# Tile 0 of x in two column parts, and the first key step between its transposes

## The chip, the cores and the metric

The kernel runs on one core of a Trainium2 chip. A core has a matrix engine (TensorE, PE in the profile; PEld is its weight load), a vector engine (VectorE, DVE), ScalarE (ACT), GpSimd (POOL) and SyncE (SP), which here only issues transfers. SP and ACT each have a queue of transfers. The metric is the device time of one execution in microseconds; before the change it is 190.84 us, the median of 5 runs (190.61 to 191.13).

## The reference

Two linear-attention blocks A and B read the same x (2048 rows, 640 columns, bf16) with weights of their own, and a gate mixes them row by row. The reference, cut to what matters:

```python
x = A_x
g = sigmoid((x * gate_w).sum(-1))
def block(x, wqkv, wo):                    # H = 32 heads of 20
    q, k, v = split_heads(x @ wqkv)
    phi = lambda t: where(t > 0, t + 1, exp(t)) + 1e-6
    pq, pk = phi(q), phi(k)
    kv, z = einsum("bhsd,bhse->bhde", pk, v), pk.sum(s)
    o = (pq @ kv) / ((pq * z).sum(-1) + 1e-6)
    return heads_joined(o) @ wo
out = g * block(x, A_wqkv, A_wo) + (1 - g) * block(x, B_wqkv, B_wo)
```

## The kernel before

x is cut into 16 tiles of 128 rows, and its 640 columns into 5 chunks of 128. The matrix engine needs x with columns on the partitions (XT), so every tile is transposed: tiles 0 and 1 on TensorE, against an identity matrix that comes with the constants (x_tp, L432 to L462: five products into PSUM, L438, in three pieces of 1, 2 and 2 columns, each followed by a copy to XT on VectorE, L453), and the tiles from 2 on by transposing transfers. The stages are: the keys of all tiles and both blocks (k_step, L485: for one tile, block and chunk a product with 512 weight columns, L491, and one with the other 128, L492; five steps make a tile's keys, then k_post applies phi), the products of keys with x (g_unit, L612), the queries (q_unit, L738), small products for the heads, and the output (o_mm, L905).

The order of the work: TensorE runs what it is given in the order written. For the other engines a planner (Sched, L75) walks through the work with estimated costs and lets each engine take, among the operations that can start, the one that can start first. It also assigns the 8 PSUM banks: a key step's result takes two neighbouring banks, a transposed piece one, the dummy products one. The first loads of a queue keep the order written (chain, L342). Each waiting operation waits for semaphores of what it needs, right before it is issued.

The start, which the change touches:

- ACT's queue (L395, L396): the constants with the identity (46 KB), then the gate's weights (1.2 KB).
- SP's queue (L397 to L413): x tile 0, key weights of A chunk 0, x tile 1, key weights of A chunks 1 to 4, then those of B, then the transposing loads, the rest of x and the other weights. Each of the first ones has 160 KB.
- TensorE (L548 to L559): six dummy products of ones with 512 columns (warm, L421), which nothing reads; the five transposes of tile 0; key step of tile 0, chunk 0; the five transposes of tile 1; the key steps of tile 0 chunk 1, tile 1 chunk 0, tile 1 chunk 1; the small transpose of the gate's weights (gate_col, L466); and then the steps of chunks 2 to 4 for both tiles.

The code of that order:

```python
    warm(6)
    pss = [Buf("k", "ps", 2) for _ in range(2)]
    x_tp(0)
    k_step("A", 0, 0, pss[0])
    x_tp(1)
    k_step("A", 0, 1, pss[0])
    k_step("A", 1, 0, pss[1])
    k_step("A", 1, 1, pss[1])
    gate_col()
```

Of the kernel before, what the change touches and what calls it, by code (L numbers as in the profile page):

```python
# [6 lines left out]
ACT = mybir.ActivationFunctionType  # L7
# [4 lines left out]
D = 640  # L12
# [62 lines left out]
class Sched:  # L75
# [7 lines left out]
    def op(self, eng, fn, cost, ins=(), outs=(), after=(), prio=None, name="", dma=None):  # L83
        o = Op(eng, fn, cost, list(ins), list(outs), after, len(self.ops) if prio is None else prio, name, dma)
        self.ops.append(o)
        return o
# [165 lines left out]
def body(nc, A_x, A_wqkv, A_wo, B_x, B_wqkv, B_wo, gate_w, out, log=None):  # L252
    x = A_x[0]
# [8 lines left out]
    XN = sb("XN", [128, NT, XS_W], bf)  # L262
# [54 lines left out]
    ONE = sb("ONE", [128, 128], bf)  # L317
# [10 lines left out]
    op = sch.op  # L328

    def psw(b, w):  # L330
        return PS[:, b.slot : b.slot + b.n, :].rearrange("p a b -> p (a b)")[:, 0:w]
# [3 lines left out]
    def dma(q, name, dst, src, nbytes, ins=(), outs=(), after=(), issue=450.0, transpose=False, prio=None):  # L335
        def fn(e):
            d = dst() if callable(dst) else dst
            with nc.allow_non_contiguous_dma(reason="layout"):
                return e.dma_start(d, src() if callable(src) else src, transpose=transpose)  # L339

        o = op(q, fn, 0.0, ins, outs, after, prio=prio, name=name, dma=(issue, nbytes, 95.0 if transpose else 330.0))
        if loading:  # L342
            o.behind = chain.get(q)
            chain[q] = o
        return o

    def mm_cost(n):
        return n / 2.4 + 2.5

    def act_cost(n):  # L350
        return 190 + 0.833 * n

    def dve1(n):
        return 155 + 1.04 * n
# [5 lines left out]
    bxn = [Buf("xn%d" % t) for t in range(NT)]  # L360
    bxt = [Buf("xt%d" % t) for t in range(NT)]
    bwk = {(X, c): Buf("wk%s%d" % (X, c)) for X in XS for c in range(NC)}
    bcst, bone, beps, bgwb = Buf("cst"), Buf("one"), Buf("eps"), Buf("gwb")
# [6 lines left out]
    bxo = Buf("xo")  # L370
    op("POOL", lambda e: e.memset(XN[:, :, D : D + 1], 1.0), 200.0, outs=[bxo], name="xones")

    def ld_x(q, t):
        dma(q, "x%d" % t, XN[:, t, 0:D], x[128 * t : 128 * t + 128, :], 163840, outs=[bxn[t]])

    def ld_wk(q, X, c, after=()):
        dma(q, "wk%s%d" % (X, c), WK[X][:, c, 0:D], wqkv[X][128 * c : 128 * c + 128, D : 2 * D], 163840, outs=[bwk[X, c]], after=after)
# [15 lines left out]

    bgw = Buf("gw5")
    dma("ACT", "cst", CST[:, :], cap[:, :], 128 * CW * 2, outs=[bcst])  # L395
    dma("ACT", "gw", GW5[:, :], gate_w.rearrange("(c p) -> c p", p=128), 1280, outs=[bgw])  # L396
    for c in range(NC):  # L397
        if c < 2:
            ld_x("SP", c)
        ld_wk("SP", "A", c)  # L400
    for c in range(NC):
        ld_wk("SP", "B", c)
# [15 lines left out]

    bw = Buf("warm", "ps")

    def warm(n):  # L421
        for i in range(n):
            op(
                "PE",
                lambda e: e.matmul(psw(bw, 512), ONE[:, :], ONE[:, :].unsqueeze(1).to_broadcast([128, 4, 128]), start=True, stop=True),
                430.0,
                ins=[bone],
                outs=[bw],
                name="warm",
            )  # L430

    def x_tp(t):  # L432
        for lo, hi in ((0, 1), (1, 3), (3, 5)):
            bt = Buf("tp", "ps")
            for c in range(lo, hi):
                op(
                    "PE",
                    lambda e, c=c, lo=lo, bt=bt: e.matmul(  # L438
                        PS[:, bt.slot, 128 * (c - lo) : 128 * (c - lo) + 128],
                        XN[:, t, 128 * c : 128 * c + 128],  # L440
                        IDN,
                        start=True,
                        stop=True,
                    ),
                    100.0,
                    ins=[bxn[t], bcst],
                    outs=[bt],
                    name="tp%d" % t,
                )
            half = Buf("xth")  # L450
            op(
                "DVE",
                lambda e, lo=lo, hi=hi, bt=bt: e.tensor_copy(  # L453
                    XT[:, lo:hi, 128 * t : 128 * t + 128],
                    PS[:, bt.slot, 0 : 128 * (hi - lo)].rearrange("p (c s) -> p c s", c=hi - lo),
                ),
                dve1(128 * (hi - lo)),
                ins=[bt],
                outs=[half],
                name="tpc%d" % t,  # L460
            )
            bxt[t].parts = getattr(bxt[t], "parts", []) + [half] * (hi - lo)  # L462
# [20 lines left out]
    bpk = {}  # L483

    def k_step(X, t, c, ps):  # L485
        w = D + 1 if X == "B" else D

        def fn(e):
            a = psw(ps, w)
            l = XT[:, c, 128 * t : 128 * t + 128]  # L490
            e.matmul(a[:, 0:512], l, WK[X][:, c, 0:512], start=(c == 0), stop=(c == NC - 1))  # L491
            return e.matmul(a[:, 512:w], l, WK[X][:, c, 512:w], start=(c == 0), stop=(c == NC - 1))  # L492

        xin = [bxt[t].parts[c] if hasattr(bxt[t], "parts") else bxt[t]]
        op(
            "PE",
            fn,
            mm_cost(512) + mm_cost(128),
            ins=xin + [bwk[X, c]] + ([bgc] if X == "B" else []),
            outs=[ps],  # L500
            name="k%s%d_%d" % (X, t, c),
        )
# [39 lines left out]
    def k_unit(X, t):  # L542
# [2 lines left out]
            k_step(X, t, c, ps)  # L545
        k_post(X, t, ps)

    warm(6)  # L548
    pss = [Buf("k", "ps", 2) for _ in range(2)]
    x_tp(0)  # L550
    k_step("A", 0, 0, pss[0])
    x_tp(1)
    k_step("A", 0, 1, pss[0])
    k_step("A", 1, 0, pss[1])
# [13 lines left out]
    for t in range(2, NT):  # L568
# [12 lines left out]
        ins=[bgg, bge2] + bge,  # L581
        outs=[bgg2],
        prio=LOW + 52,
        name="gm",
# [9 lines left out]
    for i, X in enumerate(XS):  # L594
        for j in range(NB):
# [8 lines left out]
                ins=bgd,  # L604
                outs=[b],
# [6 lines left out]
    def g_unit(X, g, fill):  # L612
        ps = Buf("g", "ps", 2)
        i = XS.index(X)
        for t in range(NT):

            def fn(e, t=t):
                a = psw(ps, D + 1)
                l = PKt[X][:, t, g::5]
                e.matmul(a[:, 0:512], l, XN[:, t, 0:512], start=(t == 0), stop=(t == NT - 1))  # L620
                return e.matmul(a[:, 512 : D + 1], l, XN[:, t, 512 : D + 1], start=(t == 0), stop=(t == NT - 1))  # L621

            op("PE", fn, mm_cost(512) + mm_cost(128), ins=[bxn[t], bxo, bpk[X, t]], outs=[ps], name="g%s%d_%d" % (X, g, t))
            if t % 4 == 3 and t < NT - 1:
                fill(t // 4)
        b, z = Buf("gt"), Buf("zbd")
        bgs[X, g] = Buf("gs%s%d" % (X, g))
        bz[X, g] = z
        op("ACT", lambda e: e.activation(GTS[X][:, g, :], psw(ps, D), ACT.Copy), act_cost(D), ins=[ps], outs=[b], name="gc")
        op(  # L630
            "DVE",
            lambda e: e.tensor_copy(ZC[:, NC * i + g : NC * i + g + 1], psw(ps, D + 1)[:, D : D + 1]),
            170.0,
            ins=[ps, b],
            outs=[z],
            name="zc",
        )
        dma(
            "SP",
            "gs%s%d" % (X, g),  # L640
            GS[X][:, :, 128 * g : 128 * g + 128],
            GTS[X][:, g, :],
            163840,
            ins=[b],
            outs=[bgs[X, g]],
            issue=850.0,
            transpose=True,
        )
# [343 lines left out]
    for g in range(NC):  # L992
        g_unit("A", g, lambda k: q_next(1))
# [28 lines left out]
    for g in range(NC):  # L1022
        g_unit("B", g, fill_b(g))
        q_next((2, 2, 1, 0, 0)[g])
# [35 lines left out]
def bass_gated_mix__linear_attn_block__linear_attn_block__prompt_kernel(nc, *args):  # L1060
    body(nc, *args)
# [28 lines left out]
```

## Time and profile before

| what | us |
|---|---|
| median of 5 runs | 190.84 (190.61 to 191.13) |
| the profiled execution's own time | 190.56 |
| its span, first to last instruction | 189.3 |
| TensorE busy | 184.3 (97%) |
| VectorE busy | 127.4 (67%) |
| ScalarE busy | 95.7 (51%) |
| first transpose of tile 0 | at 3.58 |
| first key step | at 4.37 |
| first transpose of tile 1 | at 4.98 |

The profile is of one execution. A line of the order of time gives the start, the time covered, engine, line of the kernel, operation, what is written and read, how many instructions, and in brackets how long the engine was idle before and what ended that. "SPq" and "ACTq" are the issues of transfers. A product's listed time reaches to the end of its result, so that two products in a row overlap; their pace is read from the distance of their starts. "To landing" is the time from the issue of a transfer to its last completion.

### The profile page before, as it was taken

The numbers are of one execution on the slowest core, as the hardware profiler recorded it, in microseconds if no ns is written. First come the engines' busy times: TensorE is split into PE (matmuls) and PEld (weight loads), VectorE is DVE, ScalarE is ACT, GpSimd is POOL, SyncE is SP. The second block draws the span as 40 slices with busy tenths as digits, with TensorE's granted clock in tenths as the row PEclk, the third lists the DMA queues.
The fourth block names the chain that finished last, engine by engine and source line by source line (L and its number), as shares of the span: only waits on it lengthen the run. The fifth ranks groups of instructions, "written<-read, shape, count | busy, mean of one in ns | idle before, by whom it ended". The sixth has DMA issues, their size and how long they took to land.

```text
span 189.3 us, 3195 instructions
## 1 busy us (share of the span) xinstructions
PE 184.3 (97%) x1245; PEld 107.9 (57%) x1269; DVE 127.4 (67%) x251; ACT 95.7 (51%) x171; POOL 0.4 (0%) x6
## 2 busy tenths in 40 slices
PE   7999999999999999999999999999999999999995
PEld 2555555555555566656557556655666555555552
DVE  2489888888833546478787689888996936865300
ACT  2255555656554545545584777876624875000112
POOL 0000000000000000000000000000000000000000
DMA  5979999997013011013010005430020153233222
GB/s 159 294 144 189 197 389 367 361 226 161 5 48 101 1 37 35 0 35 31 7 27 8 3 5 142 113 95 5 1 51 16 26 168 93 73 137 107 104 73 69
DMA packets 29469, 19.42 MB, mean 103 GB/s; under 512 B 17390, under 2 KB 29198, under 8 KB 29454
## 3 DMA queue, kind: packets, MB, share of 16 engines
q1 hardware_dynamic: 29300, 19.17, 38.4%
q8 instruction: 10, 0.16, 0.3%
q10 hardware_dynamic: 154, 0.05, 0.1%
q14 instruction: 5, 0.04, 0.1%
HBM read 9.95 MB, written 2.64 MB: 67 GB/s over the span
## 4 chain that ended last, share of the span: by engine, by line
PE 96%; DMA 2%; issue 1%; SPq 0%; DVE 0%; DVEq 0%
PE ps L913 23%; PE ps L743 22%; PE ps L620 18%; PE ps L491 18%; PE ps L492 5%; PE ps L621 5%; PE ps L661 2%; DMA XN<-in_A_x_dram 2%; PE ps L697 1%; SPq L339 0%; PE ps L698 0%; PE ps L826 0%; PE ps L438 0%; DVE TSB L957 0%; PE ps L472 0%
## 5 line engine op out<-in xcount | busy, mean ns | idle before, releaser
L491 PE MATMUL ps<-WKW,XT 128*128 128x512 bf16 x154 | 42.9, 379 | 0.2 <-DVE XT L453 0.2
L760 ACT ACTIVATE EK<-ps 128x512 bf16<-128x512 f32 x40 | 24.0, 599 | 31.3 <-PE ps L743 29.8
L492 PE MATMUL ps<-WKW,XT 128*128 128x128 bf16 (+1 forms) x160 | 35.1, 219 | 0.3
L524 ACT ACTIVATE EK<-ps 128x640 bf16<-128x640 f32 x32 | 22.3, 704 | 12.2 <-DVE EK L527 5.4
L491 PEld LDWEIGHTS ps<-WKW,XT 128*128 128x128 bf16 x160 | 15.6, 98 | 19.1 <-issue 0.4
L743 PE MATMUL ps<-XT,WQA 128*128 128x512 bf16 x96 | 24.0, 379 | 0.1
L743 PE MATMUL ps<-XT,WQB 128*128 128x512 bf16 x95 | 23.3, 379 | 0.4 <-issue 0.2
L620 PE MATMUL ps<-XN,PKB 128*128 128x512 bf16 x80 | 23.5, 379 | 0.0
L770 DVE TENSOR_SCALAR EK<-EK 128x512 bf16<-128x512 bf16 x40 | 11.7, 291 | 17.2 <-ACT EK L760 17.0
L620 PE MATMUL ps<-XN,PKA 128*128 128x512 bf16 x78 | 23.1, 379 | 0.1
L621 PE MATMUL ps<-XN,PKA 128*128 128x129 bf16 x80 | 17.6, 220 | 0.1
L621 PE MATMUL ps<-XN,PKB 128*128 128x129 bf16 x80 | 17.6, 220 | 0.0
L913 PE MATMUL ps<-WPA,EX 128*128 128x128 bf16 (+1 forms) x116 | 16.8, 296 | 0.2
L913 PE MATMUL ps<-WPB,PKA 128*128 128x512 bf16 (+1 forms) x118 | 16.4, 298 | 0.1
L743 PEld LDWEIGHTS ps<-XT,WQB 128*128 128x128 bf16 x100 | 10.9, 118 | 8.5 <-issue 0.2
L492 PEld LDWEIGHTS ps<-WKW,XT 128*128 128x128 bf16 x160 | 15.7, 98 | 0.0
L743 PEld LDWEIGHTS ps<-XT,WQA 128*128 128x128 bf16 x100 | 10.6, 117 | 8.1
L527 DVE TENSOR_SCALAR EK<-EK 128x640 bf16<-128x640 bf16 x32 | 10.4, 325 | 7.1 <-ACT EK L524 7.1
L959 ACT ACTIVATE TSB<-ps 128x640 bf16<-128x640 f32 (+1 forms) x4 | 2.7, 677 | 23.9 <-PE ps L913 23.9
L620 PEld LDWEIGHTS ps<-XN,PKA 128*128 128x128 bf16 x80 | 9.4, 117 | 7.9
L620 PEld LDWEIGHTS ps<-XN,PKB 128*128 128x128 bf16 x80 | 9.4, 118 | 7.8
L535 DVE SCALAR_TENSOR_TENSOR PKB<-ps,EK 128x640 bf16<-128x640 f32 x16 | 13.2, 825 | 0.6
(77 smaller groups left out, 230.9 us busy)
## 6 DMA issues: line engine op xcount, KB each, us to landing
out_dram<-TSB SPq DMA_DIRECT2D x15, 160.0 KB, 1.8
XN<-in_A_x_dram SPq DMA_DIRECT2D x1, 2240.0 KB, 9.1
WKW<-in_A_wqkv_dram SPq DMA_DIRECT2D x5, 160.0 KB, 3.2
WKW<-in_B_wqkv_dram SPq DMA_DIRECT2D x5, 160.0 KB, 3.9
WQA<-in_A_wqkv_dram SPq DMA_DIRECT2D x1, 800.0 KB, 10.7
WQB<-in_B_wqkv_dram SPq DMA_DIRECT2D x1, 800.0 KB, 13.5
WVA<-in_A_wqkv_dram SPq DMA_DIRECT2D x1, 800.0 KB, 12.8
WVB<-in_B_wqkv_dram SPq DMA_DIRECT2D x1, 800.0 KB, 14.3
```

The source lines that it names most:

```text
L491: e.matmul(a[:, 0:512], l, WK[X][:, c, 0:512], start=(c == 0), stop=(c == NC - 1))
L492: return e.matmul(a[:, 512:w], l, WK[X][:, c, 512:w], start=(c == 0), stop=(c == NC - 1))
L524: op("ACT", lambda e: e.activation(EK[:, ek.slot, :], psw(ps, D), ACT.Exp), act_cost(D), ins=[ps] + first, outs=[ek], name="ke")
L527: lambda e: e.tensor_scalar(EK[:, ek.slot, :], EK[:, ek.slot, :], 1.0, EPS, op0=ALU.min, op1=ALU.add),
L535: lambda e: e.scalar_tensor_tensor(PKt[X][:, t, :], psw(ps, D), 0.0, EK[:, ek.slot, :], op0=ALU.max, op1=ALU.add),
L620: e.matmul(a[:, 0:512], l, XN[:, t, 0:512], start=(t == 0), stop=(t == NT - 1))
L621: return e.matmul(a[:, 512 : D + 1], l, XN[:, t, 512 : D + 1], start=(t == 0), stop=(t == NT - 1))
L661: r = e.matmul(PS[0:GR, ps.slot, GR * i : GR * i + GR], WV[X][:, c, lo : lo + GR], gv[:, c, :, lo // 5 : lo // 5 + 24], start=(c == 0), st ...
L743: r = e.matmul(PS[:, ps.slot, :], WQ[X][:, c, g::5], XT[:, c, 512 * b : 512 * b + 512], start=(c == 0), stop=(c == NC - 1),)
L760: lambda e: e.activation(EQ[:, eq.slot, :], PS[:, ps.slot, :], ACT.Exp),
L770: lambda e: e.tensor_scalar(EQ[:, eq.slot, :], EQ[:, eq.slot, :], 1.0, EPS, op0=ALU.min, op1=ALU.add),
L913: r = e.matmul(a[:, l0 - lo : h0 - lo], PQ[X, b][:, g, 128 * (t % 4) : 128 * (t % 4) + 128], WP[X][:, g, l0:h0], start=(X == first and g = ...
```

## The change

Tile 0 of x is loaded in two column parts: columns 0 to 255 (64 KB) on SP's queue, in the place of the old load, and columns 256 to 639 (96 KB) on ACT's queue, between the constants and the gate's weights. The transposes of chunks 0 and 1 of tile 0 wait for the first part, those of chunks 2 to 4 for the second. Tile 0's transposes of chunks 2 to 4 are moved behind the key step of tile 0, chunk 0, and the pieces of both tiles become 1, 1 and 3 columns. Of the six dummy products four stay, and four of a quarter of the width (128 columns) follow them. The later product that reads tile 0 of x as a whole (g_unit, t = 0) is told of both parts.

```diff
     dma("ACT", "cst", CST[:, :], cap[:, :], 128 * CW * 2, outs=[bcst])
+    bx0 = Buf("xn0a")
+    dma("ACT", "x0b", XN[:, 0, 256:D], x[0:128, 256:D], 98304, outs=[bxn[0]])
+    dma("SP", "x0a", XN[:, 0, 0:256], x[0:128, 0:256], 65536, outs=[bx0])
     dma("ACT", "gw", GW5[:, :], gate_w.rearrange("(c p) -> c p", p=128), 1280, outs=[bgw])
     for c in range(NC):
-        if c < 2:
-            ld_x("SP", c)
+        if c == 1:
+            ld_x("SP", 1)
         ld_wk("SP", "A", c)
...
-    def warm(n):
+    def warm(n, w=4):
         for i in range(n):
             op(
                 "PE",
-                lambda e: e.matmul(psw(bw, 512), ONE[:, :], ONE[:, :].unsqueeze(1).to_broadcast([128, 4, 128]), start=True, stop=True),
-                430.0,
+                lambda e: e.matmul(psw(bw, 128 * w), ONE[:, :], ONE[:, :].unsqueeze(1).to_broadcast([128, w, 128]), start=True, stop=True),
+                107.0 * w,
...
-    def x_tp(t):
-        for lo, hi in ((0, 1), (1, 3), (3, 5)):
+    def x_tp(t, pieces=((0, 1), (1, 2), (2, 5))):
+        for lo, hi in pieces:
...
-                    ins=[bxn[t], bcst],
+                    ins=[bx0 if t == 0 and c < 2 else bxn[t], bcst],
...
-    warm(6)
+    warm(4)
+    warm(4, 1)
     pss = [Buf("k", "ps", 2) for _ in range(2)]
-    x_tp(0)
+    x_tp(0, ((0, 1), (1, 2)))
     k_step("A", 0, 0, pss[0])
+    x_tp(0, ((2, 5),))
     x_tp(1)
...
-            op("PE", fn, mm_cost(512) + mm_cost(128), ins=[bxn[t], bxo, bpk[X, t]], outs=[ps], name="g%s%d_%d" % (X, g, t))
+            op("PE", fn, mm_cost(512) + mm_cost(128), ins=[bxn[t], bxo, bpk[X, t]] + ([bx0] if t == 0 else []), outs=[ps], name="g%s%d_%d" % (X, g, t))
```

## The prediction

> **What bounds the kernel now.** I read the page first (busy times and the chain that ended last), then the order of time of the first six microseconds, then the stretches of half a microsecond with the DMA share, then the loads with their times to landing.
>
> ```profile
> span 189.3 us, 3195 instructions
> PE 184.3 (97%) x1245; PEld 107.9 (57%) x1269; DVE 127.4 (67%) x251; ACT 95.7 (51%) x171; POOL 0.4 (0%) x6
> PE 96%; DMA 2%; issue 1%; SPq 0%; DVE 0%; DVEq 0%
> ```
>
> TensorE is the bound nearly everywhere, and the 2% DMA of the chain lies at the start. So a change at the start is worth exactly the time by which it moves the point from which TensorE no longer waits. The order of time shows that point:
>
> ```profile
> 1.05 2.74 PE L425 MATMUL ps<-ONE 128*128 128x512 bf16 x6 [1.05 <-DVE ONE L368]
> 3.24 0.11 PEld L438 LDWEIGHTS ps<-CST,XN 128*128 128x128 bf16 x1 [0.36 <-DMA XN<-in_A_x_dram]
> 3.58 0.56 PE L438 MATMUL ps<-CST,XN 128*128 128x128 bf16 x5
> 3.94 0.95 DVE L453 CAST XT<-ps 128x128 bf16<-128x128 f32 x3 [2.94 <-PE ps L438]
> 4.37 0.38 PE L491 MATMUL ps<-WKW,XT 128*128 128x512 bf16 x1 [0.23 <-DVE XT L453]
> 4.59 0.22 PE L492 MATMUL ps<-WKW,XT 128*128 128x128 bf16 x1
> 4.97 0.28 PEld L438 LDWEIGHTS ps<-CST,XN 128*128 128x128 bf16 x5 [0.50 <-DMA XN<-in_A_x_dram]
> 4.98 0.45 PE L438 MATMUL ps<-CST,XN 128*128 128x128 bf16 x5 [0.17 <-DMA XN<-in_A_x_dram]
> 5.25 0.95 DVE L453 CAST XT<-ps 128x128 bf16<-128x128 f32 x3 [0.35 <-PE ps L438]
> 5.39 0.10 PEld L491 LDWEIGHTS ps<-WKW,XT 128*128 128x128 bf16 x1
> 5.40 0.39 PE L491 MATMUL ps<-WKW,XT 128*128 128x512 bf16 x1
> ```
>
> The five transposes of tile 0 start at 3.58, its first key step at 4.37. Then TensorE stands until x tile 1 has landed (4.97), transposes it, and stands once more before the key step of tile 0, chunk 1, whose weights load at 5.39. The five transposes of tile 1 are spaced 0.056, so they had left TensorE free from about 5.26. What came at 5.39 is the key weights of chunk 1, the fourth load of the SP queue:
>
> ```profile
> L339 SPq DMA_DIRECT2D WKW<-in_A_wqkv_dram x1: 432/432/432, 2.1 to 2.1; - x1
> DMA to landing us min/median/max: 3.2/3.2/3.2
> ```
>
> Issued at 2.12, landed 3.2 later: 5.35 or so, 0.04 before that weight load. Tile 1, issued at 1.64, landed 3.3 later, at 4.93. From 5.40 on TensorE is busy almost without a gap. So two loads of the SP queue, tile 1 and then chunk 1 of the key weights, set the end, and tile 0 doesn't.
>
> **Tile 0 in two parts.** The loads of the SP queue start 0.44 to 0.47 apart (0.74, 1.18, 1.64, 2.12). The first column part takes the old load's place and, with 128 rows as before, I give it the old issue time (0.39), so chunk 0's weights, tile 1 and chunk 1 are issued when they were. The second part goes to ACT's queue behind the constants, at 1.13. What it is moved past there: the gate weights (from 1.13 to about 1.55) and the table load (from 1.81 to about 2.25, 1.28 long). The first exponential is at 8.00; the gate weights are read at 6.32, and with the slowest of the early loads' times to landing (4.0) they would be there at 5.55. Both cost nothing; a landing later than 6.3 would cost its excess one for one.
>
> Does it move tile 1 and chunk 1? The bytes ahead of chunk 1's end are the same (46 of constants, then four times 160 KB). Stretches: length, busy time of each engine, clock, DMA share, GB/s.
>
> ```profile
> 2.00:2.50 0.50, 0.50 (x3) 0.18 (x2) 0.00 (x0) 0.50 (x1) 0.00 (x0) 1.00 0.90 276
> 2.50:3.00 0.50, 0.50 (x3) 0.15 (x1) 0.00 (x0) 0.50 (x1) 0.00 (x0) 1.00 1.05 375
> 3.00:3.50 0.50, 0.50 (x2) 0.11 (x1) 0.00 (x0) 0.10 (x1) 0.00 (x0) 1.00 1.12 159
> 3.50:4.00 0.50, 0.50 (x6) 0.38 (x4) 0.06 (x1) 0.00 (x0) 0.00 (x0) 1.00 0.62 143
> 4.00:4.50 0.50, 0.27 (x4) 0.13 (x2) 0.50 (x3) 0.00 (x0) 0.00 (x0) 1.00 0.95 318
> ```
>
> The engines are full from 2.0, and the slow stretch from 3.0 to 4.0 lies behind tile 0. Upper bound: 128 more packets, 8 for each of 16 engines, and one more completion each. In the first 9 us ACT's queue moved 154 packets, 0.05 MB, in 2.9% of 16 engines' time, 27 ns a packet; SP's moved 1961, 2.02 MB, in 75.7%, 56 ns. A line through these two (309 and 1030 bytes) leaves 15 ns for an empty packet: 9 times 15 is 0.13 us later. Lower bound: if a queue were a road of its own, SP's would carry 96 KB less ahead of tile 1, at 375 GB/s 0.26 us earlier. I take +0.1: a DMA share at or over 0.9 with 276 to 375 GB/s is what full engines look like, so packets and not queues should count.
>
> [...]
>
> **Shorter dummies.** Their starts are 0.43 apart (weight loads at 1.45, 1.88, 2.31, 2.73), so the sixth ends its issue at 3.58, just when the first transpose starts: tile 0 had landed by 3.24. Four long ones reach 2.73, four of a quarter 3.16. The first part lands between the constants' time (0.73 + 2.3 = 3.0) and the old load's (3.2). So transposes 0 and 1 start near 3.2, 0.4 earlier. The copy started 0.36 after the first transpose and the key step 0.43 after that: 3.99 now, and chunk 0's weights landed at 1.18 + 2.4 = 3.6. The key step issues in 0.28 (half pace: 0.55), the other three transposes in 0.17 (0.32): done at 4.44 (4.86). The second part, issued at 1.13, lands between 2.3 and 3.3 later, 3.4 to 4.4; at the late end the transposes end at 4.6. All are before 4.97. So the 0.4 us saved become a longer wait for tile 1: gain 0 on the path, and its cover is that wait.
>
> **Pieces and order.** Pieces of 1, 1 and 3 columns replace 1, 2 and 2. The copies took 292 and 415 ns for 128 and 256 columns, so I estimate 538 for 384. Tile 1: the three together end near 6.20 as before, and chunk 2 of tile 1 is read first at about 6.7: cost 0. Tile 0: its last copy starts some 0.27 after the last transpose, 4.66, and ends at 5.20, ahead of the copy of tile 1's first column at 5.25. In the half-pace case it ends near 5.56 and holds that copy, and so tile 1's first key step (5.68), up to 0.25: upper bound +0.2, I take 0. The wait on the first part that the diff adds to the later product of t = 0 is long over. PSUM still has a bank for every piece.
>
> **Sum.** The profiled execution took 190.56 (span 189.3 and 1.26 around it), 0.28 under the median of 190.84. 190.56 + 0.1 = 190.66; against the median 190.94, which I forecast, within 0.2% (0.38 us, about what a measurement can tell from no change). Own range: 190.84 - 0.26 to 190.84 + 0.13 + 0.2, so 190.6 to 191.2.
>
> **Rival 1, slower: TensorE's clock.** The dummies run 0.43 apart, later 512-column products 0.22; five transposes take 0.56 at 3.58 but 0.45 at 4.98. So the pace doubles inside the transposes of tile 0, some 2.8 us after the first dummy, although the granted clock reads 1.00 throughout. TensorE was busy from 1.05 to 4.1 without a break. Now it pauses from about 3.4 to 3.99. If that pause makes the doubling start anew, it comes at 3.99 + 2.8 = 6.8. The work from 5.40 to 6.8 then runs at half pace, +0.7, and tile 1's transposes end at 5.51 in place of 5.39, +0.1: with the 0.1 above 191.7. It decides if the pause comes before the doubling and is counted. For it: the doubling in the profile lies at about 3.85, inside the new pause. Against: 2.3 us of unbroken work ahead of it. [...]
>
> **Rival 2, a gain: SP's queue is relieved** and both loads land 0.26 earlier, or as fast as chunk 0's weights (2.4: 4.04 and 4.52). For it: 3.2 and 3.3 against 2.4. Even then tile 1's first copy waits behind tile 0's last (next start about 5.03 + 0.29), and tile 1's first key step can't start before 5.46 in place of 5.68: 0.22 to 0.26, 190.6. Against: the full engines.
>
> **Rival 3, the change does nothing it says:** the first part lands no earlier than 3.2 to 3.3 and the dummies only end sooner; the key step moves by 0.3. 190.8 to 190.9, since the same wait covers it.
>
> **How the numbers follow.** No net change, rival 3 included, 0.62; rival 1 0.16; rival 2 0.12; something downstream, where VectorE's and ScalarE's order is planned anew, 0.10, half each way. Rival 2's price lies within 0.2%, but its spread crosses the line: 0.07 of it counts as faster, with 0.05 of downstream 0.12. Slower: rival 1's 0.16 and 0.05, so 0.21. Same: 0.67. The range runs from 190.4 (rival 2 less the 0.2 by which the runs spread downward) to 191.8 (rival 1 and 0.1) and leaves out about 0.13.
>
> **What would show it.** Right: first transpose near 3.2, first key step near 4.0, and in front of tile 1's transposes a wait of 0.1 to 0.5 until 4.9 to 5.1; key step of chunk 1 at 5.4 to 5.55, its weights 3.2 to 3.3 after issue. Rival 1: products still 0.43 apart after 5.4. Rival 2: that key step before 5.2. The forecast is wrong if tile 1 or chunk 1 lands over 0.3 us away from 4.93 and 5.35, or the pace doubles after 5.4.

## The result, and the profile after

The changed kernel takes 192.60 us, the median of 22 runs (190.92 to 193.20); the kernel before took 190.85 in 40 runs beside them (190.49 to 191.56). The ratio is 1.0067, with a 95% interval of 1.0051 to 1.0083: slower by some 0.7%, and outside the forecast range (190.4 to 191.8). The runs of the changed kernel don't lie round one value: 7 of 22 are under 191.6, three between 191.7 and 192.2, and 12 above 192.5. Something that differs from one execution to the next is part of the answer.

The page of the profile after (this execution took 193.01, span 191.7):

```profile
span 191.7 us, 3201 instructions
PE 186.3 (97%) x1247; PEld 109.1 (57%) x1271; DVE 127.4 (66%) x251; ACT 95.6 (50%) x171; POOL 0.4 (0%) x6
PE 94%; DMA 2%; issue 1%; ACT 1%; SPq 1%; DVE 1%; ACTq 0%; DVEq 0%
```

TensorE is still the bound, and it is busy for 2.0 us longer although it has 0.43 us less of dummies. The order of time (start, time covered, engine, line, what; idle time before in brackets; lines 425, 438, 491 and 492 of the kernel before are 428, 441, 494 and 495 now; the runs below have numbers of their own, and the operation tells which line is meant):

```profile
1.05 2.31 PE L428 MATMUL ps<-ONE 128*128 128x512 bf16 x8 [1.05 <-DVE ONE L368]
...
3.16 0.42 PE L441 MATMUL ps<-CST,XN 128*128 128x128 bf16 x2
...
4.36 0.61 PE L494 MATMUL ps<-WKW,XT 128*128 128x512 bf16 x1 [0.78 <-DMA WKW<-in_A_wqkv_dram]
...
4.87 1.06 PE L441 MATMUL ps<-CST,XN 128*128 128x128 bf16 x8
...
6.01 0.10 PEld L494 LDWEIGHTS ps<-WKW,XT 128*128 128x128 bf16 x1 [0.36 <-DMA WKW<-in_A_wqkv_dram]
6.02 0.61 PE L494 MATMUL ps<-WKW,XT 128*128 128x512 bf16 x1
...
6.53 0.63 PE L494 MATMUL ps<-WKW,XT 128*128 128x512 bf16 x1
```

Two things are to be seen. First, the transposes start at 3.16 as planned, but the first key step comes at 4.36, no earlier than before (4.37), since chunk 0's key weights are late; and the key step of chunk 1 comes at 6.02 in place of 5.40, since chunk 1's are late too. Second, a 512-column product covers 0.61 to 0.63 and its successor starts 0.40 to 0.43 later; before it was 0.38 and 0.22. TensorE still runs at half pace, and it goes on so until 10.0:

```profile
9.42 0.63 PE L494 MATMUL ps<-WKW,XT 128*128 128x512 bf16 x1
9.85 0.30 PE L495 MATMUL ps<-WKW,XT 128*128 128x128 bf16 x1
9.95 0.41 PE L494 MATMUL ps<-WKW,XT 128*128 128x512 bf16 x1
10.20 0.22 PE L495 MATMUL ps<-WKW,XT 128*128 128x128 bf16 x1
10.26 0.38 PE L494 MATMUL ps<-WKW,XT 128*128 128x512 bf16 x1
```

In the profile before, the pace doubled at 3.83, inside the transposes of tile 0 (their starts are 0.11, 0.11, 0.07 and 0.06 apart). The granted clock reads 1.00 in both profiles, so only the distance of the starts tells.

The load of chunk 1's weights (issued at 2.15), and the stretches in which it came (last two columns: DMA share, GB/s):

```profile
L339 SPq DMA_DIRECT2D WKW<-in_A_wqkv_dram x1: 432/432/432, 2.1 to 2.1; - x1
...
DMA to landing us min/median/max: 3.8/3.8/3.8
```

```profile
2.00:2.50 0.50, 0.50 (x3) 0.18 (x2) 0.00 (x0) 0.24 (x1) 0.00 (x0) 1.00 1.05 174
2.50:3.00 0.50, 0.50 (x5) 0.26 (x3) 0.00 (x0) 0.50 (x1) 0.00 (x0) 1.00 0.41 110
3.00:3.50 0.50, 0.50 (x6) 0.31 (x3) 0.00 (x0) 0.50 (x1) 0.00 (x0) 1.00 1.06 363
3.50:4.00 0.50, 0.08 (x1) 0.00 (x0) 0.49 (x2) 0.04 (x1) 0.00 (x0) 1.00 1.18 373
4.00:4.50 0.50, 0.14 (x1) 0.13 (x2) 0.00 (x1) 0.00 (x0) 0.00 (x0) 1.00 0.86 220
4.50:5.00 0.50, 0.50 (x4) 0.24 (x3) 0.00 (x0) 0.00 (x0) 0.00 (x0) 1.00 0.52 61
```

Before, the engines moved 276 and 375 GB/s from 2.0 to 3.0 and dipped once ahead of chunk 1, from 3.0 to 4.0 (159 and 143). Now there is a dip from 2.3 to 2.9 (8 to 177 GB/s in stretches of 0.1), right behind the short first part, and a second from 4.3 to 5.2 (38 to 179). Chunk 0's weights took 3.1 from issue to landing in place of 2.4, chunk 1's 3.8 in place of 3.2. Tile 1 itself was there at 4.70, earlier than before (4.93).

**The sum.** From the first key step that can run on (that of chunk 1) to the doubling, half of the time is lost. So the time should be 190.56 + (start of that key step - 5.40) + half of the time from there to the doubling. For the profile after: 0.62 and (10.03 - 6.02) / 2 = 2.00, 193.18 against 193.01 measured. In this execution about a quarter of the 2.62 is the loads, the rest the late doubling. The experiments are there to tell what makes each of the two.

### The profile page after: what moved, and what is told of

Its sections match the earlier page's. It is cut to its first block, busy times and chain, and to the rows that moved or that the text cites. A ratio compares the mean times of both kernels' runs of the same rounds, so it can differ in the third digit from the quotient of the medians.

```text
span 191.7 us, 3201 instructions
## 1 busy us (share of the span) xinstructions
PE 186.3 (97%) x1247; PEld 109.1 (57%) x1271; DVE 127.4 (66%) x251; ACT 95.6 (50%) x171; POOL 0.4 (0%) x6
## 4 chain that ended last, share of the span: by engine, by line
PE 94%; DMA 2%; issue 1%; ACT 1%; SPq 1%; DVE 1%; ACTq 0%; DVEq 0%
PE ps L918 23%; PE ps L748 22%; PE ps L625 17%; PE ps L494 17%; PE ps L626 5%; PE ps L495 5%; DMA WKW<-in_A_wqkv_dram 2%; PE ps L666 2%; PE ps L702 1%; ACT EK L527 1%; SPq L339 1%; PE ps L831 0%; DVE EK L530 0%; PE ps L703 0%; ACT GE L520 0%
## 5 line engine op out<-in xcount | busy, mean ns | idle before, releaser
L494 PE MATMUL ps<-WKW,XT 128*128 128x512 bf16 x154 | 44.9, 392 | 0.9 <-DMA WKW<-in_A_wqkv_dram 0.8
L495 PE MATMUL ps<-WKW,XT 128*128 128x128 bf16 (+1 forms) x160 | 35.9, 224 | 0.3
L494 PEld LDWEIGHTS ps<-WKW,XT 128*128 128x128 bf16 x160 | 16.0, 100 | 20.9 <-DMA WKW<-in_A_wqkv_dram 1.4
L625 PE MATMUL ps<-XN,PKB 128*128 128x512 bf16 x76 | 22.6, 379 | 0.0
L918 PE MATMUL ps<-WPA,EX 128*128 128x512 bf16 (+1 forms) x117 | 16.8, 297 | 0.2
L495 PEld LDWEIGHTS ps<-WKW,XT 128*128 128x128 bf16 x160 | 16.0, 100 | 0.0
L538 DVE SCALAR_TENSOR_TENSOR PKA<-ps,EK 128x640 bf16<-128x640 f32 x16 | 13.2, 825 | 0.6
```

The source lines that it names most:

```text
L538: lambda e: e.scalar_tensor_tensor(PKt[X][:, t, :], psw(ps, D), 0.0, EK[:, ek.slot, :], op0=ALU.max, op1=ALU.add),
L918: r = e.matmul(a[:, l0 - lo : h0 - lo], PQ[X, b][:, g, 128 * (t % 4) : 128 * (t % 4) + 128], WP[X][:, g, l0:h0], start=(X == first and g = ...
```

## The experiments

The first four, run together (kernel before beside them: 190.98, 33 runs, 190.69 to 191.77), take the change apart. Theory 1 was the clock, theory 2 the loads.

**Six long dummies in the changed kernel.**

```diff
-    warm(4)
-    warm(4, 1)
+    warm(6)
```

> The changed kernel with the six long dummy products of the kernel before in place of four long and four short ones. Theory 1 (clock): the doubling of TensorE's pace, at about 3.85 in the profile before and at 9.95 in the profile after, is missed because TensorE pauses ahead of it; 0.43 us more of dummies leaves a pause of about 0.55 instead of 1.09 in front of the first key step, so the doubling comes before 5.4 in most executions: 190.9 to 191.4, and less spread than 190.9 to 193.2. Theory 2 (loads): chunk 0's and chunk 1's key weights land 0.6 to 0.7 later because of the split load, and TensorE waits for them whatever its pace: at least 191.4, and the doubling late or early by chance as in the changed kernel, up to 192.6.

Measured: 191.32 (191.12 to 193.06, 11 runs), ratio 1.0023 (0.9999 to 1.0047). Nine runs lie from 191.12 to 191.49, two above 193. In its profile chunk 1's weights land at 6.01, as late as in the changed kernel, and the doubling is at 6.21, inside the first of these products:

```profile
6.05 0.46 PE L494 MATMUL ps<-WKW,XT 128*128 128x512 bf16 x1
...
6.40 0.38 PE L494 MATMUL ps<-WKW,XT 128*128 128x512 bf16 x1
```

So longer dummies take most of the long times away and leave the loads where they are: the median is in theory 1's range, the loads are as theory 2 had them.

**Short dummies alone in the kernel before.**

```diff
-    warm(6)
+    warm(4)
+    warm(4, 1)
```

> The kernel before with the four long and four short dummy products of the change, nothing else. Theory 1: the five transposes of tile 0 follow the dummies at 3.2 to 3.3 without a pause and the key step comes at 4.0 to 4.1, so that only the wait for tile 1 grows, from 0.17 to about 0.6; some executions miss the doubling: 190.9 to 191.6 in the median, spread above that of before. If the length of the dummies in front of the transposes is all that counts, 192.6 as in the changed kernel. Theory 2: 190.85, spread as before.

Measured: 191.18 (190.77 to 192.66, 11 runs), ratio 1.0034 (1.0007 to 1.0061): six runs from 190.77 to 191.18 and five from 192.40 to 192.66, with nothing between. Theory 2's 190.85 with the spread of before fell. The profile is of one of the slow ones:

```profile
3.20 0.71 PE L438 MATMUL ps<-CST,XN 128*128 128x128 bf16 x5
3.97 0.58 PE L491 MATMUL ps<-WKW,XT 128*128 128x512 bf16 x1
...
5.16 0.71 PE L438 MATMUL ps<-CST,XN 128*128 128x128 bf16 x5 [0.50 <-DMA XN<-in_A_x_dram]
5.67 0.63 PE L491 MATMUL ps<-WKW,XT 128*128 128x512 bf16 x1
```

The loads are those of before (chunk 1 at 5.53), the first key step comes 0.4 earlier, and the head start becomes a wait for tile 1, as the prediction had it. But the pace doubles at 9.66 only. The dummies alone cost 1.4 to 1.7 us over the median of before, in five of eleven executions.

**The pause filled.** The changed kernel with eight quarter dummies behind tile 0's first two transposes.

```diff
     x_tp(0, ((0, 1), (1, 2)))
+    warm(8, 1)
     k_step("A", 0, 0, pss[0])
```

> The changed kernel with eight more quarter dummies (0.86 us at half pace) behind tile 0's first two transposes, where TensorE paused from 3.27 to 4.36. Theory 1: the doubling comes early again: 190.9 to 191.3, spread as before. Theory 2: the loads are as late as in the changed kernel: 191.4 or more.

Measured: 191.45 (191.10 to 191.65, 11 runs), ratio 1.0018 (1.0008 to 1.0029).

```profile
3.37 0.83 PE L428 MATMUL ps<-ONE 128*128 128x128 bf16 x8
4.06 0.39 PE L494 MATMUL ps<-WKW,XT 128*128 128x512 bf16 x1
...
6.03 0.39 PE L494 MATMUL ps<-WKW,XT 128*128 128x512 bf16 x1 [0.84 <-DMA WKW<-in_A_wqkv_dram]
```

The doubling is back at 3.84 (the product at 4.06 covers 0.39), all the times above 191.65 are gone, and what is left, 0.15 to 0.55 by the interval, is the wait for chunk 1's weights, here 0.84 in front of 6.03. This run separates the two causes: filling the pause removes the one and leaves the other.

**The split load alone.** The kernel before, its dummies, pieces and order, with tile 0 in two column parts on the two queues; every transpose of tile 0 waits for both. The loads are those of the change; beside them:

```diff
-                    ins=[bxn[t], bcst],
+                    ins=([bx0, bxn[0]] if t == 0 else [bxn[t]]) + [bcst],
```

> The kernel before with tile 0 loaded as two column parts on the two queues; all five transposes wait for both parts, dummies, pieces and order of TensorE are those of before. Theory 1: 190.8 to 191.0, since the dummies reach to 3.58 and tile 0 is there by then or little later. Theory 2: chunk 0 and chunk 1 land at about 4.3 and 6.0 as in the profile after: 191.4 to 191.5 with early doubling.

Measured: 192.57 (191.09 to 193.30, 11 runs), ratio 1.0066 (1.0038 to 1.0093): the whole loss of the change, with none of its dummies and none of its order.

```profile
4.46 0.69 PE L441 MATMUL ps<-CST,XN 128*128 128x128 bf16 x5 [0.67 <-DMA XN<-in_A_x_dram]
...
6.43 0.61 PE L494 MATMUL ps<-WKW,XT 128*128 128x512 bf16 x1
```

Tile 0 as a whole is there at 4.33 in place of 3.20, chunk 1's weights at 6.39, and TensorE, its dummies done at 3.6, stands until 4.46; the pace doubles at 8.86. Theory 1 as I had put it (190.8 to 191.0, tile 0 there by 3.58) fell: it had the loads on time. Both causes act, and the loads feed the other one: a late load makes a pause (0.67 here), and with a pause the doubling came late (8.86; 3.84 in e3, whose pause was filled).

Four more (kernel before beside them: 191.24, 35 runs, 190.75 to 191.70 and two near 193). The first two ask what makes the loads late: theory Q, two queues side by side; theory S, short first parts. Both build on the filled version, so that the pace shouldn't matter.

**Both parts on SP's queue.**

```diff
-    dma("ACT", "x0b", XN[:, 0, 256:D], x[0:128, 256:D], 98304, outs=[bxn[0]])
     dma("SP", "x0a", XN[:, 0, 0:256], x[0:128, 0:256], 65536, outs=[bx0])
+    dma("SP", "x0b", XN[:, 0, 256:D], x[0:128, 256:D], 98304, outs=[bxn[0]])
```

> The kernel of e3_pause_filled (changed kernel, pause filled with eight quarter dummies) with both column parts of tile 0 on SP's queue, one behind the other. In e3 chunk 0's key weights were there at 4.01 and chunk 1's at 5.98, in the profile before at 3.56 and 5.35. Theory Q (two queues that load side by side hold each other up): without the second queue chunk 1 comes at 5.35 to 5.6, time 190.8 to 191.1. Theory S (the first parts are short: the 16 engines have moved them by 2.4 and run dry before the next load is up to speed): parts are as short as before and every later load is issued 0.47 later: chunk 0 at 4.1 or later, chunk 1 at 5.9 or later, time 191.4 or more.

Measured: 191.30 (191.02 to 191.64, 11 runs), ratio 0.9998 (0.9972 to 1.0024). Chunk 0 at 4.50, chunk 1 at 5.61, although issued at 2.6. Chunk 0 is as theory S said, chunk 1 as the end of theory Q's range; neither is carried whole.

**The second part ahead of the constants.**

```diff
+    dma("ACT", "x0b", XN[:, 0, 256:D], x[0:128, 256:D], 98304, outs=[bxn[0]])
     dma("ACT", "cst", CST[:, :], cap[:, :], 128 * CW * 2, outs=[bcst])
-    dma("ACT", "x0b", XN[:, 0, 256:D], x[0:128, 256:D], 98304, outs=[bxn[0]])
```

> The kernel of e3_pause_filled with the second column part ahead of the constants on ACT's queue, so that both parts of tile 0 (160 KB) are the first thing on the engines and the constants follow. Theory Q: still two queues side by side: chunk 1's weights at 5.9 to 6.0, 191.4. Theory S: the engines have work until 2.6 as in the kernel before: chunk 0 at 3.6 and chunk 1 at 5.35 to 5.6; the transposes wait for the constants until 3.4 to 3.5, which the wait for tile 1 hides: 190.8 to 191.1.

Measured: 191.84 (191.13 to 193.21, 11 runs), ratio 1.0034 (1.0007 to 1.0060). Chunk 1's weights come early, at 5.12, with two queues side by side: theory Q falls. The parts are as short as in the change, and still chunk 1 isn't late: it took 3.0 from issue to landing, where the changed kernel's took 3.8. Chunk 0's come at 4.39, not at 3.6, and the constants took 3.0 to land, as the chain of waits shows (start, length, what):

```profile
1.15 3.04 DMA CST<-kconsts
4.33 0.37 PE ps L441 x2
```

So TensorE stood from 3.16 to 4.33 and the pace doubled at 7.96. Theory S got chunk 0 and the constants wrong, and its chunk 1 (5.35 to 5.6) came earlier than it said.

**Chunk 0's key weights on ACT's queue, in the kernel before.** Tile 0 stays whole.

```diff
+    ld_wk("ACT", "A", 0)
     dma("ACT", "gw", GW5[:, :], gate_w.rearrange("(c p) -> c p", p=128), 1280, outs=[bgw])
...
-        ld_wk("SP", "A", c)
+        if c:
+            ld_wk("SP", "A", c)
```

> The kernel before with A's key weights of chunk 0 on ACT's queue behind the constants; tile 0 whole and first on SP's queue, tile 1 and chunk 1 issued 0.46 earlier there (1.18 and 1.64). If the issue from one queue holds the loads back, chunk 1 lands 0.3 to 0.45 earlier, 190.5 to 190.6. If the engines are full (as the prediction had it), chunk 1 lands at 5.3 to 5.4 as before, 190.85 to 190.98. Theory Q: two queues side by side, chunk 1 0.4 to 0.6 later, 191.4.

Measured: 190.83 (190.63 to 191.44, 12 runs), ratio 0.9981 (0.9963 to 1.0000). Chunk 1, issued at 1.65 and so 0.47 earlier, lands at 4.81 in place of 5.35 to 5.7; chunk 0 at 4.52.

```profile
L339 SPq DMA_DIRECT2D WKW<-in_A_wqkv_dram x1: 432/432/432, 1.6 to 1.6; - x1
...
DMA to landing us min/median/max: 3.2/3.2/3.2
```

The engines weren't full in the sense in which I had used the word: an earlier issue brought an earlier landing. The key step of chunk 1 still starts at 5.35, because now the first key step waits for chunk 0 (4.66) and tile 1's transposes stand behind it.

**The kernel before with its pauses filled.**

```diff
     x_tp(0)
+    warm(4, 1)
     k_step("A", 0, 0, pss[0])
+    warm(4, 1)
     x_tp(1)
```

> The kernel before with four quarter dummies in front of the first key step and four behind it, so that TensorE pauses for no more than about 0.2 us from 1.05 to 5.4; the loads are untouched. Clock: the kernel before has times up to 191.77, 0.8 over its median, as if the doubling came after 5.4 in some executions. If pauses delay it, the spread falls to 190.5 to 191.1 and the median to 190.7 to 190.9. [...] Where the pace is still half, the dummies cost up to 0.2 in front of tile 1's transposes.

Measured: 191.08 (190.79 to 191.60, 12 runs), ratio 0.9996 (0.9976 to 1.0015). Median and spread stay as they were, within the noise. TensorE worked without a break from 1.05, and still:

```profile
6.04 0.63 PE L491 MATMUL ps<-WKW,XT 128*128 128x512 bf16 x1
6.47 0.31 PE L492 MATMUL ps<-WKW,XT 128*128 128x128 bf16 x1
6.57 0.48 PE L491 MATMUL ps<-WKW,XT 128*128 128x512 bf16 x1
6.89 0.22 PE L492 MATMUL ps<-WKW,XT 128*128 128x128 bf16 x1
```

The doubling came at 6.77, after 5.7 us of unbroken work, where the profile before needed 2.8. So it isn't a count of unbroken work that starts anew after a pause. What sets the place of the doubling instead, none of these runs shows. Theory W, which two expectations below name, was a guess of mine at it, and it wasn't shown.

**Three long dummies in the kernel before** (run with the next one; kernel before beside them 191.03, 16 runs, 190.68 to 191.37). The loads are untouched, so this tests the clock alone.

```diff
-    warm(6)
+    warm(3)
```

> The kernel before with three long dummies in place of six, nothing else: TensorE pauses from 2.33 to about 3.27, the loads are untouched. [...] Theory N (the doubling starts anew after a pause and needs 2.8 us, as the prediction's first rival had it): always at about 6.1, 191.0 to 191.4 with little spread.

Measured: 192.10 (191.63 to 193.46, 6 runs), ratio 1.0071 (1.0044 to 1.0098), 0.6 to 2.4 over the kernel before: theory N, with 191.0 to 191.4, is out. The profile, of the fastest run:

```profile
3.15 0.71 PE L438 MATMUL ps<-CST,XN 128*128 128x128 bf16 x5 [0.63 <-DMA XN<-in_A_x_dram]
...
5.69 0.58 PE L491 MATMUL ps<-WKW,XT 128*128 128x512 bf16 x1
...
7.14 0.31 PE L492 MATMUL ps<-WKW,XT 128*128 128x128 bf16 x1
```

It still runs at half pace at 7.14 (0.31 for 128 columns, 0.22 at full pace) and at full pace from 7.38. So the doubling is late again, after a pause of 0.63 in front of tile 0's transposes and one of 0.40 in front of tile 1's. The three dummies, 1.3 us of work that nothing reads, are worth 1.1 us between the medians (0.8 to 1.9 by the interval, from six runs).

**Another order, and chunk 0's weights on ACT's queue.** f3 with tile 1's transposes ahead of the first key step, tile 1's first key step ahead of the one that needs chunk 1, and four quarter dummies between the transposes.

```diff
     x_tp(0)
-    k_step("A", 0, 0, pss[0])
+    warm(4, 1)
     x_tp(1)
-    k_step("A", 0, 1, pss[0])
+    k_step("A", 0, 0, pss[0])
     k_step("A", 1, 0, pss[1])
+    k_step("A", 0, 1, pss[0])
     k_step("A", 1, 1, pss[1])
```

> The kernel before with A's key weights of chunk 0 on ACT's queue (as f3), four quarter dummies behind tile 0's transposes, and tile 1's transposes and first key step ahead of what waits for chunk 1's weights. In f3 tile 1 landed at 4.33, chunk 0 at 4.52 and chunk 1 at 4.81. The sum of two terms (when the key steps can run on, and half of the time from there to the doubling): key steps run on from 4.65 to 5.0 instead of 5.40, so 190.2 to 190.5 with an early doubling; the stretches of theory W still pass at the same times as in the kernel before, so its spread of about 0.8 upward stays: median 190.4 to 190.8, 0.2 to 0.4 below f3 and 0.4 to 0.7 below the kernel before.

Measured: 190.81 (190.32 to 191.50, 11 runs), ratio 0.9985 (0.9972 to 0.9998): faster than the kernel before by little, and than the changed kernel by 1.8 us. It is at the upper end of what was expected (190.4 to 190.8); that it would beat f3 by 0.2 to 0.4 fell, the two can't be told apart.

```profile
4.55 0.74 PE L440 MATMUL ps<-CST,XN 128*128 128x128 bf16 x5
5.08 0.63 PE L493 MATMUL ps<-WKW,XT 128*128 128x512 bf16 x1
...
6.10 0.38 PE L493 MATMUL ps<-WKW,XT 128*128 128x512 bf16 x1
```

TensorE has no pause left ahead of the doubling at 6.04, and that doubling is what costs now, (6.04 - 5.08) / 2 = 0.48. In the two profiles of the kernel before, the first above and the second below, the pace doubles at 3.83 and 6.82; I estimate that the same range would be worth 0 to 0.87 here ((6.82 - 5.08) / 2), a part of the spread of 1.2 us.

**Both kernels once more**, for a second profile of each.

> The changed kernel once more, for a second profile. If the split load is what makes the weights late, chunk 1 is there at 5.9 to 6.4 again, as in the four profiles with the split load on two queues behind the constants (5.97, 6.01, 5.98, 6.39); if that was chance, near 5.35 to 5.7. The time follows the two-term sum: 190.56 + (start of that key step - 5.40) + half of the time from there to the doubling, within 0.2.

> The kernel before once more, for a second profile: chunk 1 at 5.35 to 5.7 as in the three profiles with tile 0 loaded whole on SP's queue (5.35, 5.53, 5.70), doubling between 3.5 and 7.0 by theory W, and the time by the same sum within 0.2.

Measured: the changed kernel 192.80, chunk 1 at 5.85, its key step at 5.90, doubling at 9.72; the kernel before 191.41, chunk 1 at 5.58, key step at 5.74, doubling at 6.82. Chunk 1's 5.85 is just below what I had written. The sums give 192.97 and 191.44. The second profile of the kernel before, still at half pace where the first was at full pace since 3.83:

```profile
5.74 0.63 PE L491 MATMUL ps<-WKW,XT 128*128 128x512 bf16 x1
...
6.27 0.63 PE L491 MATMUL ps<-WKW,XT 128*128 128x512 bf16 x1
...
6.80 0.39 PE L491 MATMUL ps<-WKW,XT 128*128 128x512 bf16 x1
```

**What of the split makes the loads late?** Two more kernels, profiled twice each, as e4 (split load alone, order and dummies of before). One cuts at column 512 in place of 256, so that the first part has 128 KB and the second 32; the other cuts by rows, 64 and 64.

```diff
+    dma("ACT", "x0b", XN[:, 0, 512:D], x[0:128, 512:D], 32768, outs=[bxn[0]])
+    dma("SP", "x0a", XN[:, 0, 0:512], x[0:128, 0:512], 131072, outs=[bx0])
```

> The kernel of e4_split_only (kernel before, tile 0 in two column parts on the two queues) with the cut at column 512 in place of 256: 128 KB on SP's queue, 32 KB on ACT's. In e4 chunk 0 came at 4.5 and chunk 1 at 6.4, with the whole tile at 3.4 to 4.0 and 5.35 to 5.7. If a short first part is what makes them late, the weights come as with the whole tile: chunk 0 by 4.0, chunk 1 at 5.35 to 5.7. If any second load on ACT's queue does it: chunk 0 at 4.2 or later, chunk 1 at 5.85 or later.

> The same kernel as h1_wide_first_a once more, for a second profile: the same numbers.

```diff
+    dma("ACT", "x0b", XN[64:128, 0, 0:D], x[64:128, :], 81920, outs=[bxn[0]])
+    dma("SP", "x0a", XN[0:64, 0, 0:D], x[0:64, :], 81920, outs=[bx0])
```

> The kernel of e4_split_only with tile 0 cut by rows, 64 on SP's queue and 64 on ACT's, 80 KB each: packets of 1280 bytes as in the whole tile, 128 in all. If the narrow packets (512 and 768 bytes, twice as many) make the weights late, chunk 0 comes by 4.0 and chunk 1 at 5.35 to 5.7. If a short first part or a second load on ACT's queue does it: chunk 0 at 4.2 or later, chunk 1 at 5.85 or later.

> The same kernel as h2_rows_a once more, for a second profile: the same numbers.

Measured: cut at column 512, 190.94 and 190.83, chunk 0 at 4.08 and 3.60, chunk 1 at 5.75 and 5.60, beside 190.86 for the kernel before. That is the whole tile's range or 0.05 over it (chunk 0 at 3.56 to 4.03, chunk 1 at 5.35 to 5.70): in these two executions, with a long first part, the loss is gone, and a second load on ACT's queue is not enough to make it. Cut by rows, 192.79 and 192.94, chunk 0 at 4.51 and 4.56, chunk 1 at 6.10 and 6.22, doubling at 9.44 and 9.62. But here the issue of the first half took 0.61 in place of 0.39, and chunk 1 was issued 0.40 later (2.55 against 2.15). From its issue it took 3.6:

```profile
L339 SPq DMA_DIRECT2D WKW<-in_A_wqkv_dram x1: 432/432/432, 2.5 to 2.5; - x1
...
DMA to landing us min/median/max: 3.6/3.6/3.6
```

In the second execution it took 3.7, against 3.2 to 3.6 with the whole tile and 3.7 to 4.2 with the cut at column 256. So some two thirds of its lateness is the issue, and the cut by rows leaves open what packets of 1280 bytes do for chunk 1. Chunk 0 took 3.1, against 2.4 to 2.8 with the whole tile.

Issued at 2.12 to 2.15, chunk 1 is clearly late only with 64 KB first on SP's queue and the rest behind the constants on ACT's: 5.85 to 6.39 in five profiles (changed twice, e1, e3, e4), against 5.35 to 5.70 in five with the whole tile (before twice, e2, f4, g1). A short first part alone doesn't do it: f1 and f2 have the same parts, and chunk 1 at 5.61 (issued 0.47 later) and 5.12. Why the engines dip for half a microsecond behind the first part, and a second time later, these runs don't show. The dip's cause stays open.

All the profiles but that of g2, whose order is another, in one table (us; "doubling" from the starts of the products, within 0.1, and somewhere inside a pause for f1 and the first h1):

| kernel | key step of chunk 1 | doubling | sum | measured |
|---|---|---|---|---|
| before | 5.40 | 3.83 | 190.56 | 190.56 |
| before again | 5.74 | 6.82 | 191.44 | 191.41 |
| changed | 6.02 | 10.03 | 193.18 | 193.01 |
| changed again | 5.90 | 9.72 | 192.97 | 192.80 |
| e1 six dummies | 6.05 | 6.21 | 191.29 | 191.28 |
| e2 short dummies | 5.67 | 9.66 | 192.82 | 192.66 |
| e3 pause filled | 6.03 | 3.84 | 191.19 | 191.18 |
| e4 split only | 6.43 | 8.86 | 192.81 | 192.66 |
| f1 one queue | 5.65 | 4.1 to 4.6 | 190.81 | 191.02 |
| f2 part first | 6.74 | 7.96 | 192.51 | 192.48 |
| f3 weights on ACT | 5.35 | 4.94 | 190.51 | 190.63 |
| f4 before filled | 6.04 | 6.77 | 191.57 | 191.55 |
| g1 three dummies | 5.69 | 7.38 | 191.70 | 191.63 |
| h1 wide first | 5.80 | 3.2 to 4.4 | 190.96 | 190.94 |
| h1 again | 5.64 | 4.14 | 190.81 | 190.83 |
| h2 rows | 6.15 | 9.44 | 192.96 | 192.79 |
| h2 again | 6.27 | 9.62 | 193.11 | 192.94 |

Two terms give these 17 times within 0.21 us. For g2 the formula as it stands gives 191.26 for a measured 190.96. There the work runs on from 5.08 with one key step (0.27 at full pace) still to do that the others have behind them: counted from there, 190.56 + (5.35 - 5.40) + (6.04 - 5.08) / 2 = 190.99.

## Why the prediction was wrong

- **What bounds the start** was right: chunk 1's weights, not tile 0, set the point from which TensorE runs on, and tile 0's head start became a wait (e2, the first key step at 3.97 and tile 1's transposes at 5.16).
- **"Does it move tile 1 and chunk 1?"** is the first step that failed. I took +0.1, between -0.26 and +0.13. In the two profiles after, the key step of chunk 1 stands at 6.02 and 5.90 against 5.40 and 5.74 before, some 0.4 on average. The packet count was the wrong measure: it allowed for 0.13 at most, and the cut at column 512, with as many packets and the same bytes and queues, costs nearly nothing (190.94 and 190.83, beside 190.86). I had read the engines as full from 2.0, though the prediction's own row from 3.5 to 4.0 has a DMA share of 0.62; now they moved 110 GB/s from 2.5 to 3.0 where it was 375, and f3 landed chunk 1 earlier by issuing it earlier. What made the dip stays open.
- **"The key step ... 3.99 now"** failed by the same thing: chunk 0's weights landed at 4.31, and the pause in front of the first key step grew from the 0.6 of the prediction (3.4 to 3.99) to 1.0 (3.38 to 4.36).
- **The clock, at nothing in the sum,** is the step that failed by most: 2.0 of the 2.6 in the profile after. **Rival 1** had it, given 0.16. It was right in the main (a pause ahead of the doubling; with the pause filled, e3 doubled at 3.84) and wrong in its form: the doubling doesn't start anew 2.8 us after a pause. f4 worked for 5.7 without a break before it doubled, and in the profiles after the pace doubled at 10.0 and 9.7 where the rival had 6.8, so 2.0 in place of 0.8. The chance was mis-set as well. I had one profile of before and took its 3.83 for the kernel's; the second has 6.82. So its place changes from one execution to the next, and a kernel with a pause can pay in most of them: of the changed kernel's 22 runs, 15 took over 191.6. Theory W, by which the expectations of g2 and g4 go, no run shows; what the runs showed is a doubling at 6.04 and a spread of 1.2 us for g2, and a doubling at 6.82 for g4.
- **Shorter dummies at cost 0**, covered by the wait for tile 1: the cover holds for the path, and not for the clock. Alone they lost nothing in six runs and 1.4 or more in five.
- **Pieces and order** and the gate's weights at 0: nothing in the runs speaks against it; e3 has them all, and in its profile the wait for the weights accounts for the time within 0.01.

## What to carry to other kernels

Before a first load is cut up to bring its beginning forward, look at what lands last at the start, and at what the long load hides: here a first part of 64 KB, with the rest behind the constants on the other queue, delayed the loads that counted (chunk 1 at 5.85 to 6.39 in place of 5.35 to 5.70). Dummy products at the start can be worth time although nothing reads them and data aren't there yet: here three fewer cost 1.1 us between the medians (g1), and four of the six with four short ones behind them 1.4 to 1.7 us in five of eleven executions (e2). After taking some away, or leaving a pause behind them, look at the distance of the starts until the pace has doubled, and at the spread of the runs, not at one profile. A sum of two terms, when the real work can run on and half of the time from there to the doubling, was enough to tell the two losses apart in every profile with this order of work.

## What was not expected of the hardware

TensorE's pace doubled anywhere between 3.8 and 10.0 us although its dummies began at 1.05 in all of these kernels, and once after 5.7 us of unbroken work (f4). The granted clock read 1.00 all the while. Filling the pause of the changed kernel went with an early doubling (3.84 in e3, against 10.03 and 9.72), filling those of the kernel before did not (6.77 in f4, against 3.83 and 6.82). What sets the place, these runs don't show. The doubling of the kernel before between 3.5 and 7.0 was expected ahead of a run and came (g4, 6.82), but a doubling by 7.0 gives no more than 191.36 to 191.53 by the sum, with the key step at 5.40 to 5.74, and so doesn't account for the two runs of the kernel before near 193 (192.98 and 193.38), of which there is no profile. In the cut by rows the issue of a load with 64 rows took longer (0.61) than that of one with 128 in the profile before (0.39).
